# Block-sparse attention followed by a gated feed-forward layer: scores of two heads in two 64-row halves of TensorE, the mask as a 0/1 product, the hidden layer kept on the chip, and the two layers interleaved by token group

## The chip, the cores and the metric

One core of one Trainium2 chip runs the whole program. The metric is device time of one execution in microseconds (us), the median of several runs; nearly all runs of a kernel lie within 0.8% of its median. Every ratio below is the ratio of a kernel's fast runs to the fast runs of the kernel before, of the same rounds on the same chip, so it is not quite the ratio of the medians that are quoted. Differences in us between two experiments or to the changed kernel are differences of medians, and the experiments ran on three chips; where the ratios give a figure more than 1 us away, the text says so. A profile is one execution; its span is 1 to 2 us shorter than the timed run, and stage times below are read from profiles.

Engines: PE is TensorE (PEld its weight loads), DVE is VectorE, ACT is ScalarE, POOL is GpSimd, SP is SyncE, which here only issues transfers.

## The reference

Batch 4, 8 heads, 768 positions, head size 64. The mask works on blocks of 32 positions: neighbours, first and last block, and three sampled blocks per block row. The second layer is called MoE in the code, but it is one dense gated layer.

```python
scores = scale * np.matmul(q, k.transpose(0, 1, 3, 2))      # (4, 8, 768, 768)
mask = np.abs(blk_i - blk_j) <= 1
mask = mask | (blk_i == 0) | (blk_j == 0) | (blk_i == n_blocks - 1) | (blk_j == n_blocks - 1)
for qb in range(n_blocks):
    for kb in sampled_blocks[qb]:
        mask[qb*32:(qb+1)*32, kb*32:(kb+1)*32] = True
scores = np.where(mask, scores, -1e9)
attn = softmax(scores)                                      # written out in the reference
x = (attn @ v) as 3072 tokens x 512
h = x @ w_in                                                # 512 -> 2048
g = h * (1.0 / (1.0 + np.exp(-beta * h)))
return g @ w_out                                            # 2048 -> 512
```

Both kernels skip the maximum (the scores are small), sum each row of exp by a column of ones beside v, and compute the gate as 0.5 * h * (1 + tanh(beta*h/2)).

## The kernel before

One head at a time. q and k are transposed on PE into the first 64 rows of a tile; 24 more rows hold the block mask (-30000 for a masked block on the q side, a one-hot of the key's block on the k side). The score matmul thus contracts 88 rows and gives masked scores, and exp is all that follows.

```python
CROWS = D + NB                                   # 64 + 24
for kc in range(NKC):                            # 6 chunks of 128 keys
    sc = scores_pool.tile([P, S], FP32, tag="sc")
    nc.tensor.matmul(sc[:, 0:512], lhsT=ka[0:CROWS, kc*P:(kc+1)*P],
                     rhs=qa[0:CROWS, 0:512], start=True, stop=True)
    nc.tensor.matmul(sc[:, 512:S], lhsT=ka[0:CROWS, kc*P:(kc+1)*P],
                     rhs=qa[0:CROWS, 512:S], start=True, stop=True)
    nc.scalar.activation(out=et[:, kc, :], in_=sc, func=AF.Exp, bias=0.0, scale=SCALE)
```

The hidden layer is computed in two halves. "Front" matmuls of the first three token groups run between the heads; VectorE casts their result and it goes to DRAM. "Back" reads it again, takes tanh on ScalarE and the gate product on VectorE. In the source the rest of the layer stands after attention; in the trace 46 of the 96 tanh run before the last rows of attention are written.

```python
def emit_h_front(tg, ffc, h_pool):
    ...                                          # four matmuls of 512 columns into hp
    nc.vector.tensor_copy(out=hst, in_=hp)
    nc.sync.dma_start(out=h_dram[tg * N_FFC + ffc], in_=hst)

def emit_h_back(tg, ffc, g_sb):
    nc.sync.dma_start(out=hld, in_=h_dram[tg * N_FFC + ffc])
    nc.scalar.activation(out=t_sb, in_=hld, func=AF.Tanh, bias=0.0, scale=beta_h_sb[:, ffc:ffc+1])
    nc.vector.scalar_tensor_tensor(out=g_sb[:, ffc, :], in0=t_sb, scalar=1.0, in1=hld,
                                   op0=ALU.add, op1=ALU.mult)
```

The instructions are traced in this order, but the build's scheduler fixes each engine's queue with its own model of durations.

The softmax here doesn't subtract the row's maximum and nothing guards it: scores larger than these inputs give would overflow.

Of the kernel before, what the change touches and what calls it, by code (L numbers as in the profile page):

```python
# [9 lines left out]
FP32 = mybir.dt.float32  # L11
FP16 = mybir.dt.float16
AF = mybir.ActivationFunctionType
ALU = mybir.AluOpType

NEG = -30000.0
# [3 lines left out]
def kernel(  # L20
# [17 lines left out]
    NKC = S // P  # L38
    NQC = S // P
# [3 lines left out]
    N_DMC = D_MODEL // P  # L43
    N_FFC = D_FF // P
    SCALE = 1.0 / float(D) ** 0.5

    CROWS = D + NB

    n_bh = B * H
    N_TG = N_TOK // 512  # L50

    persist = ctx.enter_context(tc.tile_pool(name="persist", bufs=1))
    setup_pool = ctx.enter_context(tc.tile_pool(name="setup", bufs=1))
    dram_pool = ctx.enter_context(tc.tile_pool(name="dram", bufs=1, space=bass.MemoryType.DRAM))


    h_dram = dram_pool.tile([N_TG * N_FFC, P, 512], FP16, name="h_dram")

    identity = persist.tile([P, P], FP16, name="identity")
    make_identity(nc, identity)  # L60

    xT_sb = persist.tile([P, N_DMC, N_TOK], FP16, name="xT_sb")
    w_in_sb = persist.tile([P, N_DMC, D_FF], FP16, name="w_in_sb")
    w_out_sb = persist.tile([P, N_FFC, D_MODEL], FP16, name="w_out_sb")
    beta_h_sb = persist.tile([P, N_FFC], FP32, name="beta_h_sb")

    sb_i32 = setup_pool.tile([NB, 3], mybir.dt.int32, name="sb_i32")
# [3 lines left out]
    nc.sync.dma_start(out=sb_i32, in_=sb_lo)  # L71
    sb_f32 = setup_pool.tile([NB, 3], FP32, name="sb_f32")
    nc.vector.tensor_copy(out=sb_f32, in_=sb_i32)

    mask_blk = setup_pool.tile([NB, NB], FP32, name="mask_blk")
    nc.vector.memset(mask_blk, 1.0)
    nc.gpsimd.affine_select(out=mask_blk, in_=mask_blk, pattern=[[-1, NB]],
                            compare_op=ALU.is_ge, fill=0.0, base=1,
                            channel_multiplier=1)
    nc.gpsimd.affine_select(out=mask_blk, in_=mask_blk, pattern=[[1, NB]],  # L80
                            compare_op=ALU.is_ge, fill=0.0, base=1,
                            channel_multiplier=-1)
    nc.gpsimd.affine_select(out=mask_blk, in_=mask_blk, pattern=[[0, NB]],
                            compare_op=ALU.not_equal, fill=1.0, base=0,
                            channel_multiplier=1)
    nc.gpsimd.affine_select(out=mask_blk, in_=mask_blk, pattern=[[0, NB]],
                            compare_op=ALU.not_equal, fill=1.0, base=-(NB - 1),
                            channel_multiplier=1)
    nc.gpsimd.affine_select(out=mask_blk, in_=mask_blk, pattern=[[1, NB]],
                            compare_op=ALU.not_equal, fill=1.0, base=0,  # L90
                            channel_multiplier=0)
    nc.gpsimd.affine_select(out=mask_blk, in_=mask_blk, pattern=[[1, NB]],
                            compare_op=ALU.not_equal, fill=1.0, base=-(NB - 1),
                            channel_multiplier=0)
    iota_j = setup_pool.tile([NB, NB], FP32, name="iota_j")
    nc.gpsimd.iota(iota_j, pattern=[[1, NB]], base=0, channel_multiplier=0,
                   allow_small_or_imprecise_dtypes=True)
    for r in range(3):
        ind_r = setup_pool.tile([NB, NB], FP32, name=f"ind_{r}")
        nc.vector.tensor_scalar(out=ind_r, in0=iota_j, scalar1=sb_f32[:, r:r + 1],  # L100
                                scalar2=None, op0=ALU.is_equal)
        nc.vector.tensor_tensor(out=mask_blk, in0=mask_blk, in1=ind_r, op=ALU.max)

    mask_add16 = setup_pool.tile([NB, NB], FP16, name="mask_add16")
    nc.vector.tensor_scalar(out=mask_add16, in0=mask_blk, scalar1=1.0, scalar2=-NEG,
                            op0=ALU.subtract, op1=ALU.mult)

    with tc.tile_pool(name="setup_psum", bufs=1, space=bass.MemoryType.PSUM) as setup_psum:
        maskT_ps = setup_psum.tile([NB, NB], FP16, name="maskT_ps")
        nc.tensor.transpose(out=maskT_ps, in_=mask_add16, identity=identity[0:NB, 0:NB])  # L110
        maskT16 = setup_pool.tile([NB, NB], FP16, name="maskT16")
        nc.vector.tensor_copy(out=maskT16, in_=maskT_ps)  # L112

    beta_sb = setup_pool.tile([P, N_FFC], FP32, name="beta_sb")
    nc.scalar.dma_start(out=beta_sb, in_=moe_beta.rearrange("(c p) -> p c", p=P))
# [5 lines left out]
    weight_chunks = []  # L121
    for c in range(N_DMC):
        weight_chunks.append((w_in_sb[:, c, :], w_in_r[:, c, :], None,
                              "w_in_st", [P, D_FF]))
    for c in range(N_FFC // 2):
        weight_chunks.append((w_out_sb[:, 2 * c:2 * c + 2, :],
                              w_out_r[:, 2 * c:2 * c + 2, :], 0.5,
                              "w_out_st", [P, 2, D_MODEL]))
    wstage = ctx.enter_context(tc.tile_pool(name="wstage", bufs=2))

    NBUF = 3
    NEBUF = 2

    qaug_tiles = []
    kaug_tiles = []
    vaug_tiles = []
    et_tiles = []
    for i in range(NBUF):
        qa = persist.tile([P, S], FP16, name=f"qaug_{i}")
        ka = persist.tile([P, S], FP16, name=f"kaug_{i}")  # L140
        va = persist.tile([P, NKC, D + 1], FP16, name=f"vaug_{i}")
        nc.vector.tensor_copy(
            out=qa[D:CROWS, :].rearrange("p (i w) -> p i w", w=BLK),
            in_=maskT16[:, :].to_broadcast([NB, NB, BLK]),
        )
        nc.vector.memset(ka[D:CROWS, :], 1.0)
        nc.gpsimd.affine_select(out=ka[D:CROWS, :], in_=ka[D:CROWS, :],
                                pattern=[[1, NB], [0, BLK]],
                                compare_op=ALU.is_equal, fill=0.0, base=0,
                                channel_multiplier=-1)  # L150
        nc.vector.memset(va[:, :, D:D + 1], 1.0)
        qaug_tiles.append(qa)
        kaug_tiles.append(ka)
        vaug_tiles.append(va)
    for i in range(NEBUF):
        et = persist.tile([P, NKC, S], FP16, name=f"et_{i}")
        et_tiles.append(et)

    stage_pool = ctx.enter_context(tc.tile_pool(name="stage", bufs=2))
    xstage_pool = ctx.enter_context(tc.tile_pool(name="xstage", bufs=2))  # L160

    attn_psum_ctx = ExitStack()
    scores_pool = attn_psum_ctx.enter_context(
        tc.tile_pool(name="scores_psum", bufs=2, space=bass.MemoryType.PSUM))
    tp_pool = attn_psum_ctx.enter_context(
        tc.tile_pool(name="tp_psum", bufs=2, space=bass.MemoryType.PSUM))
    av_pool = attn_psum_ctx.enter_context(
        tc.tile_pool(name="av_psum", bufs=1, space=bass.MemoryType.PSUM))
    xtp_pool = tp_pool
    hf_pool = attn_psum_ctx.enter_context(  # L170
        tc.tile_pool(name="hf_psum", bufs=1, space=bass.MemoryType.PSUM))

    moe_sbuf = ctx.enter_context(tc.tile_pool(name="moe_sbuf", bufs=3))

    small_pool = ctx.enter_context(tc.tile_pool(name="small", bufs=4))

    xstage = None

    def emit_h_front(tg, ffc, h_pool):
        hp = h_pool.tile([P, 512], FP32, tag="hfp", name="hfp")  # L180
        for c in range(N_DMC):
            nc.tensor.matmul(hp,  # L182
                             lhsT=w_in_sb[:, c, ffc * P:(ffc + 1) * P],
                             rhs=xT_sb[:, c, tg * 512:(tg + 1) * 512],
                             start=(c == 0), stop=(c == N_DMC - 1))
        hst = moe_sbuf.tile([P, 512], FP16, tag="hst", name="hst")
        nc.vector.tensor_copy(out=hst, in_=hp)  # L187
        nc.sync.dma_start(out=h_dram[tg * N_FFC + ffc], in_=hst)

    def emit_h_back(tg, ffc, g_sb):  # L190
        hld = moe_sbuf.tile([P, 512], FP16, tag="hld", name="hld")
        nc.sync.dma_start(out=hld, in_=h_dram[tg * N_FFC + ffc])
        t_sb = moe_sbuf.tile([P, 512], FP16, tag="t_sb", name="t_sb")
        nc.scalar.activation(out=t_sb, in_=hld, func=AF.Tanh,  # L194
                             bias=0.0, scale=beta_h_sb[:, ffc:ffc + 1])
        nc.vector.scalar_tensor_tensor(out=g_sb[:, ffc, :], in0=t_sb,  # L196
                                       scalar=1.0, in1=hld,
                                       op0=ALU.add, op1=ALU.mult)

    def emit_o_unit(tg, tsub, o_pool, g_sb):  # L200
        op = o_pool.tile([P, D_MODEL], FP32, tag="op", name="op")
        for ffc in range(N_FFC):
            nc.tensor.matmul(op,  # L203
# [175 lines left out]
```

## Time and profile before

| | before |
|---|---|
| median time, first 3 runs | 362.66 us (361.95 to 363.61) |
| span of the profile | 361.5 us |
| first exp starts | 26.4 us |
| last rows of attention written | 233.7 us |

The first lines are from the profile's page: busy time of each engine, and the chain of work that ended last, by engine.

```profile
PE 326.7 (90%) x2785; PEld 184.5 (51%) x2785; DVE 238.1 (66%) x488; ACT 206.5 (57%) x289; POOL 4.9 (1%) x16
...
PE 80%; ACT 9%; DMA 5%; DVE 3%; issue 1%; SPq 0%; ACTq 0%
```

TensorE is busy for 90% of the time and is 80% of the chain.

The next lines are the page's costliest groups: line, engine, operation, what it writes from what, shapes and count, then busy us and mean ns of one, then idle time of the engine just before them and what ended it.

```profile
L194 ACT ACTIVATE t_sb<-hld,beta_h_sb 128x512 f16<-128x512 f16 x96 | 66.7, 720 | 66.6 <-DMA hld<-h_dram 39.6
L182 PE MATMUL hfp<-xT_sb,w_in_sb 128*128 128x512 f16 x384 | 100.7, 379 | 0.0
L203 PE MATMUL op<-w_out_sb,g_sb 128*128 128x512 f16 x384 | 84.7, 379 | 0.0
L272 ACT ACTIVATE et_142<-sc 128x768 f16<-128x768 f32 x96 | 70.8, 812 | 23.1 <-PE sc L269 17.9
...
L187 DVE CAST hst<-hfp 128x512 f16<-128x512 f32 x96 | 64.2, 685 | 9.2 <-PE hfp L182 5.2
```

ScalarE waits 39.6 us for the hidden layer to come back from DRAM, but ScalarE is not the engine that bounds.

The table of stretches follows: the stretch, its length, busy time of each engine with its number of instructions, granted clock, DMA share and GB/s.

```profile
0.00:26.40 26.40, 5.06 (x34) 3.57 (x35) 11.69 (x34) 1.33 (x2) 4.88 (x16) 1.00 0.91 271
26.40:90.00 63.60, 57.20 (x616) 37.31 (x615) 33.96 (x82) 47.15 (x63) 0.00 (x0) 0.97 0.56 148
90.00:217.00 127.00, 125.33 (x1391) 78.11 (x1388) 102.33 (x227) 109.55 (x157) 0.00 (x0) 1.00 0.66 172
```

In the first 26.4 us nothing much runs while transfers fill 91% of the DMA engines. From 90 to 217 us PE is full (125.33 of 127 us).

### The profile page before, as it was taken

To read this page: it belongs to the slowest core of one execution; us is meant where nothing else is said; L and a number is where in the kernel's file an instruction comes from. 1 tells how busy PE (TensorE), PEld (TensorE's weight loads), DVE (VectorE), ACT (ScalarE), POOL (GpSimd) and SP (SyncE) were. 2 spreads that over 40 slices of the span, in tenths; PEclk is the share of its full clock that TensorE was granted. 3 is DMA by queue.
4 is the path that set the end of the run, shared out by engine and by line. 5 is a ranking of instruction groups with operands and counts; after the bars stand their busy time and mean duration, and the time that the engine had idled before them with its cause. 6 is when DMAs were issued, how large, how long until landed. Compare 5 with 4: busy or idle time off the path is not lost.

```text
span 361.5 us, 7349 instructions
## 1 busy us (share of the span) xinstructions
PE 326.7 (90%) x2785; PEld 184.5 (51%) x2785; DVE 238.1 (66%) x488; ACT 206.5 (57%) x289; POOL 4.9 (1%) x16
## 2 busy tenths in 40 slices
PE   0329988989999999999999998999999999999995
PEld 0215655655566566566666655544444444444442
DVE  2465346555877977977887797725987977985121
ACT  0027686687889889788888977610452452443000
POOL 5000000000000000000000000000000000000000
PEclk9999989999999999999999999999999999999999
DMA  7894276655667666676666742233664754763212
GB/s 231 242 339 98 80 190 204 189 127 144 169 177 190 179 160 179 160 184 174 175 174 164 189 138 61 90 103 133 213 205 145 230 183 160 220 200 119 87 58 89
DMA packets 111303, 59.22 MB, mean 164 GB/s; under 512 B 81060, under 2 KB 105636, under 8 KB 110756
## 3 DMA queue, kind: packets, MB, share of 16 engines
q1 hardware_dynamic: 106452, 50.35, 50.1%
q10 hardware_dynamic: 4816, 8.40, 6.7%
q8 instruction: 22, 0.36, 0.4%
q14 instruction: 13, 0.11, 0.1%
HBM read 39.85 MB, written 18.87 MB: 162 GB/s over the span
## 4 chain that ended last, share of the span: by engine, by line
PE 80%; ACT 9%; DMA 5%; DVE 3%; issue 1%; SPq 0%; ACTq 0%
PE hfp L182 23%; PE op L203 23%; PE sc L266 12%; PE av L285 8%; PE tp L254 7%; ACT et_142 L272 6%; PE sc L269 5%; ACT et_141 L272 3%; DMA st_318<-in_q_dram 3%; DMA st_181<-in_k_dram 2%; PE xtp L304 2%; DVE xstage L294 1%; ACT t_sb L194 0%; SPq L71 0%; DVE recip L293 0%
## 5 line engine op out<-in xcount | busy, mean ns | idle before, releaser
L194 ACT ACTIVATE t_sb<-hld,beta_h_sb 128x512 f16<-128x512 f16 x96 | 66.7, 720 | 66.6 <-DMA hld<-h_dram 39.6
L182 PE MATMUL hfp<-xT_sb,w_in_sb 128*128 128x512 f16 x384 | 100.7, 379 | 0.0
L203 PE MATMUL op<-w_out_sb,g_sb 128*128 128x512 f16 x384 | 84.7, 379 | 0.0
L272 ACT ACTIVATE et_142<-sc 128x768 f16<-128x768 f32 x96 | 70.8, 812 | 23.1 <-PE sc L269 17.9
L272 ACT ACTIVATE et_141<-sc 128x768 f16<-128x768 f32 x96 | 70.3, 816 | 11.2 <-PE sc L269 11.0
L196 DVE SCALAR_TENSOR_TENSOR g_sb<-t_sb,hld 128x512 f16<-128x512 f16 x96 | 64.0, 684 | 11.8 <-ACT t_sb L194 11.5
L187 DVE CAST hst<-hfp 128x512 f16<-128x512 f32 x96 | 64.2, 685 | 9.2 <-PE hfp L182 5.2
L203 PEld LDWEIGHTS <-g_sb 128*128 128x128 f16 x384 | 37.6, 98 | 45.3
L182 PEld LDWEIGHTS <-w_in_sb 128*128 128x128 f16 x384 | 35.6, 97 | 35.4 <-issue 0.4
L208 DVE COPY osb<-op 128x512 f32<-128x512 f32 x24 | 16.5, 689 | 31.7 <-PE op L203 31.6
L285 PEld LDWEIGHTS <-et_142 128*128 128x128 f16 x576 | 29.2, 101 | 12.2 <-issue 1.7
L293 DVE RECIPROCAL recip<-av 128x6 f32<-128x6 f32 x32 | 6.3, 196 | 41.1 <-PE av L285 40.4
L285 PEld LDWEIGHTS <-et_141 128*128 128x128 f16 x576 | 26.3, 100 | 9.3 <-issue 2.5
L266 PE MATMUL sc<-qaug_120,kaug_121 88*128 88x512 f16 x66 | 25.8, 399 | 3.1 <-ACT et_142 L272 1.2
L266 PE MATMUL sc<-qaug_127,kaug_128 88*128 88x512 f16 x66 | 26.5, 410 | 2.1 <-ACT et_142 L272 1.2
L266 PE MATMUL sc<-qaug_134,kaug_135 88*128 88x512 f16 x60 | 23.2, 394 | 2.0 <-ACT et_142 L272 0.9
L269 PE MATMUL sc<-qaug_127,kaug_128 88*128 88x256 f16 x66 | 19.2, 291 | 0.0
L269 PE MATMUL sc<-qaug_120,kaug_121 88*128 88x256 f16 x66 | 18.8, 284 | 0.0
L294 DVE TENSOR_TENSOR xstage<-av,recip 128x384 f16<-128x384 f32 x32 | 17.6, 551 | 0.1
L269 PE MATMUL sc<-qaug_134,kaug_135 88*128 88x256 f16 x60 | 16.8, 281 | 0.0
L272 ACT ACT_TABLE_LOAD x1 | 1.3, 1283 | 22.4 <-DVE maskT_111 L112 22.4
L285 PE MATMUL av<-vaug_122,et_141 128*128 128x65 f16 x216 | 12.9, 203 | 0.0
(284 smaller groups left out, 260.7 us busy)
## 6 DMA issues: line engine op xcount, KB each, us to landing
h_dram<-hst SPq DMA_DIRECT2D x96, 128.0 KB, 1.9
hld<-h_dram SPq DMA_DIRECT2D x96, 128.0 KB, 2.3
out_dram<-osb SPq DMA_DIRECT2D x24, 256.0 KB, 2.0
w_in_st<-in_moe_w_in_dram ACTq DMA_DIRECT2D x4, 1024.0 KB, 7.1
w_out_st<-in_moe_w_out_dram ACTq DMA_DIRECT2D x8, 512.0 KB, 5.4
st_169<-in_q_dram SPq DMA_DIRECT2D x1, 192.0 KB, 8.8
st_181<-in_k_dram SPq DMA_DIRECT2D x1, 192.0 KB, 9.0
vst_193<-in_v_dram SPq DMA_DIRECT2D x1, 192.0 KB, 9.0
```

Source lines behind the costliest of these rows:

```text
L182: nc.tensor.matmul(hp, lhsT=w_in_sb[:, c, ffc * P:(ffc + 1) * P], rhs=xT_sb[:, c, tg * 512:(tg + 1) * 512], start=(c == 0), stop=(c == N_D ...
L187: nc.vector.tensor_copy(out=hst, in_=hp)
L194: nc.scalar.activation(out=t_sb, in_=hld, func=AF.Tanh, bias=0.0, scale=beta_h_sb[:, ffc:ffc + 1])
L196: nc.vector.scalar_tensor_tensor(out=g_sb[:, ffc, :], in0=t_sb, scalar=1.0, in1=hld, op0=ALU.add, op1=ALU.mult)
L203: nc.tensor.matmul(op, lhsT=g_sb[:, ffc, tsub * P:(tsub + 1) * P], rhs=w_out_sb[:, ffc, :], start=(ffc == 0), stop=(ffc == N_FFC - 1))
L208: nc.vector.tensor_copy(out=osb, in_=op)
L254: nc.tensor.transpose(out=tp[:, c, :], in_=st16[:, c, :], identity=identity[:, 0:P])
L266: nc.tensor.matmul(sc[:, 0:512], lhsT=ka[0:CROWS, kc * P:(kc + 1) * P], rhs=qa[0:CROWS, 0:512], start=True, stop=True)
L269: nc.tensor.matmul(sc[:, 512:S], lhsT=ka[0:CROWS, kc * P:(kc + 1) * P], rhs=qa[0:CROWS, 512:S], start=True, stop=True)
L272: nc.scalar.activation(out=et[:, kc, :], in_=sc, func=AF.Exp, bias=0.0, scale=SCALE)
L285: nc.tensor.matmul(av[:, qc, :], lhsT=pet[:, kc, qc * P:(qc + 1) * P], rhs=pva[:, kc, :], start=(kc == 0), stop=(kc == NKC - 1))
L294: nc.vector.tensor_tensor(out=xstage[:, :, (ph % 2) * D:(ph % 2 + 1) * D], in0=av[:, :, 0:D], in1=recip[:, :].to_broadcast([P, NQC, D]), o ...
```

## The change

Its intent: halve TensorE's work on scores by running two heads side by side in the upper and lower 64 rows of the array, halve the q and k transposes by transposing two heads at once, drop the DRAM round trip and the casts with it, and spread the feed-forward work over the attention of the next token group so that no engine idles. The mask rows no longer fit (two heads fill 128 rows), so the mask becomes a 0/1 product on VectorE after exp. The core of the diff:

```diff
-        sc = scores_pool.tile([P, S], FP32, tag="sc")
-        nc.tensor.matmul(sc[:, 0:512], lhsT=ka[0:CROWS, ...], rhs=qa[0:CROWS, 0:512], ...)
-        nc.tensor.matmul(sc[:, 512:S], lhsT=ka[0:CROWS, ...], rhs=qa[0:CROWS, 512:S], ...)
-        nc.scalar.activation(out=et[:, kc, :], in_=sc, func=AF.Exp, ...)
+        sc = sc_pool.tile([P, 2, 512], FP32, tag="sc", name="sc")
+        for i in range(kn):                       # 1 chunk of 512 queries, or 2 of 256
+            for hh in range(2):                   # head hh in rows hh*64 .. hh*64+63
+                nc.tensor.matmul(sc[:, hh, i*n:(i+1)*n],
+                                 lhsT=kT[hh*D:(hh+1)*D, (kc0+i)*P:(kc0+i+1)*P],
+                                 rhs=qT[hh*D:(hh+1)*D, q0:q0+n], start=True, stop=True)
+        et = et_pool.tile([P, 2, kn, n], FP16, tag="et", name="et")
+        nc.scalar.activation(out=et.rearrange("p h i n -> p h (i n)"), in_=sc, func=AF.Exp, ...)
+        for hh in range(2):
+            nc.vector.tensor_tensor(out=et[:, hh], in0=et[:, hh],
+                                    in1=mask_sb[:, kc0:kc0+kn, q0:q0+n], op=ALU.mult)
...
-        nc.vector.tensor_copy(out=hst, in_=hp)
-        nc.sync.dma_start(out=h_dram[tg * N_FFC + ffc], in_=hst)
-        nc.sync.dma_start(out=hld, in_=h_dram[tg * N_FFC + ffc])
-        nc.scalar.activation(out=t_sb, in_=hld, func=AF.Tanh, ...)
-        nc.vector.scalar_tensor_tensor(out=g_sb[:, ffc, :], in0=t_sb, scalar=1.0, in1=hld, ...)
+        nc.scalar.activation(out=t_sb[:, 0:n], in_=hp[:, 0:n], func=AF.Tanh, ...)
+        nc.vector.scalar_tensor_tensor(out=g[:, f, 0:n], in0=t_sb[:, 0:n], scalar=1.0,
+                                       in1=hp[:, 0:n], op0=ALU.add, op1=ALU.mult)
...
+    # beta: loaded by ScalarE's queue after the sampled blocks, scaled on VectorE
+    nc.scalar.dma_start(out=sb_i32, in_=sb_lo)
+    nc.scalar.dma_start(out=beta_sb, in_=moe_beta.rearrange("(c p) -> p c", p=P))
+    nc.vector.tensor_scalar(out=beta_h_sb, in0=beta_sb, scalar1=0.5, ...)
+    # weights: cast to fp16 by the transfer itself, issued from GpSimd
+    nc.gpsimd.dma_start(out=w_in_sb[:, :, i*512:(i+1)*512], in_=w_in_r[:, :, i*512:(i+1)*512])
...
+    tiles = [(0, 0, 256), (0, 256, 512), (1, 0, 512), (1, 512, 256),
+             (2, 0, 256), (2, 256, 512), (3, 0, 512), (3, 512, 256)]
+    groups = [[0], [1], [2], [3, 4], [5], [6], [7]]
+    # attention steps of group g are interleaved with the MoE steps of group g-1
```

Attention now goes by tiles of 256 or 512 queries. PSUM holds two score tiles of two banks, one bank for the weighted sums, and three banks shared by transposes, hidden layer and output.

## The prediction

> **What bounds the kernel now.** TensorE. The page gives PE 326.7 of 361.5 us busy (90%), the chain that ended last is 80% PE. VectorE has 238.1 us, ScalarE 206.5 us. The first exp runs only at 26.35 us (timeline), behind 192 KB loads that took about 9 us beside the weight loads. Start-to-start in the timeline: 512-column matmul 0.216 us, AV matmul 0.036, 128-column q/k transpose 0.066. PE work by these: MoE 768 x 0.216 = 166 us, scores 192 x 0.32 = 61, AV 1152 x 0.036 = 42, q/k transposes 384 x 0.066 = 25, xtp 6: 300 us.
>
> **What the change does on PE.** Two heads share a transpose: 25 to about 12 us. Score pairs run side by side: 288 matmuls of 512 columns' worth (or twice as many of 256), 61 us in series, 31 if the halves overlap fully. The Trainium skill, "TensorE: Matmul & The Clock Gate" (Part 3), measured 3.07x for four row tiles, so two should overlap nearly; but "TensorEngine Tiling (Array Packing)" (Key Properties) says changing the tiling mode drains the array, and this happens twice per score step, 144 steps. I allow 0.05 to 0.15 us per step (an estimate): scores 40 to 52 us. No run so far shows it. New PE sum: about 270 to 280 us.
>
> **VectorE.** Removed: 96 hst casts (64 us), weight casts (10 us). Added: 288 fp16 products of 512 columns; from 551 ns for 384 fp32 columns, and two elements a cycle for fp16 ("VectorE: DVE Perf Modes", perf-mode tier table), I estimate 0.42 us each, 0.34 back to back: about 100 us. Sum about 240 to 260 us: no relief.
>
> **ScalarE.** 144 exps of 1024 columns, from 0.812 us per 768 an estimated 1.03 us each (148 us busy), tanh about 60, output copies 14: about 220 us. The DRAM spill goes, but DMA was not the bound.
>
> **By stage.** All three engines are near balance, so I expect coupling losses: a bank of the hidden layer is held through tanh and gate product, and three banks serve h, o and transposes. Start to first exp about 17 us; group 0 (no MoE, VectorE-bound) 20; group 1 about 33; four full groups 47 to 50 each (first half VectorE-bound by gate plus mask, second half PE-bound); group 6 about 37; tail MoE of 256 tokens about 17. Sum about 316 us. The gain is the saved PE work (about 25 us), the earlier start (about 9 us) and fewer stalls.
>
> **Prediction: 315 us, 8 in 10 between 294 and 337.** Faster by over 2%: 0.95; within 2%: 0.03; slower: 0.02.
>
> **What would show the steps right or wrong.** Pairs of score matmuls starting within about 0.02 us of each other, with a visible gap after them before the next full-height matmul; mask products near 0.42 us; exp near 1.03 us; busy time PE 270 to 290, VectorE 240 to 260, ScalarE 210 to 230; steady groups of 47 to 50 us with VectorE above 90% in their first halves; first exp near 17 us.
>
> **What would make it wrong.** Mask products at one element a cycle (0.68 us: 75 us more on VectorE, no gain left); score halves that do not overlap or drains of 0.3 us a switch (20 to 40 us more); weight loads issued from GpSimd that come late and stall the first MoE group; or, the other way, no drain and good overlap, near 295 us.

## More of the kernel before

Note that busy time counts a matmul from its start to its modelled end, so it holds pipeline latency as well as work.

A matmul of 512 columns shows 379 ns because of that latency. Between the starts of two neighbours there are only 216 ns, and that is what a full PE pays.

## The result and the profile after

| | before | after |
|---|---|---|
| median, same rounds | 362.31 us (361.23 to 363.61) | 353.34 us (352.87 to 353.95) |
| ratio | | 0.9749 (0.9722 to 0.9776) |
| span of the profile | 361.5 us | 351.1 us |
| first exp starts | 26.4 us | 26.5 us |

The change is faster by 2.5%. The prediction was 315 us, at most 337: the direction was right and most of the gain did not come. The page of the kernel after, the lines that answer to those above:

```profile
PE 302.9 (86%) x2670; PEld 152.1 (43%) x2670; DVE 250.6 (71%) x666; ACT 216.4 (62%) x281; POOL 9.7 (3%) x26
...
PE 61%; ACT 16%; DVE 11%; DMA 7%; issue 4%; ACTq 0%
...
L215 ACT ACTIVATE et<-sc 128x1024 f16<-128x1024 f32 x144 | 143.1, 1033 | 86.4 <-PE sc L209 85.3
L218 DVE TENSOR_TENSOR et<-et,mask_sb 128x512 f16<-128x512 f16 x288 | 108.9, 420 | 30.6 <-ACT et L215 28.5
L292 PE MATMUL op<-w_out_sb,g 128*128 128x512 f16 x384 | 97.4, 380 | 0.0
...
L209 PE MATMUL sc<-qT,kT 64*128 64x256 f16 (+1 forms) x384 | 63.1, 351 | 11.0 <-ACT et L215 8.0
...
L135 DVE TENSOR_SCALAR beta_h_sb<-beta_sb 128x16 f32<-128x16 f32 x1 | 0.2, 174 | 16.5 <-DMA beta_sb<-in_moe_beta_dram 16.5
```

VectorE and ScalarE are as predicted, product by product: 420 ns, 1033 ns, 250.6 and 216.4 us busy. The last line is one that I did not foresee: a 174 ns instruction with 16.5 us of idle VectorE in front of it.

By stage. A group ends where its last attention rows are written to `xT_sb`; group 0 has no MoE work beside it, groups 2 to 5 are the four full ones, the tail is the MoE work of the last group. The scheduler runs some scores of a group before the last rows of the one before, so the borders are a little soft. First what the table of stretches gives (columns as above):

```profile
0.00:26.50 26.50, 2.08 (x19) 1.78 (x20) 5.42 (x19) 1.28 (x1) 9.70 (x26) 1.00 1.07 230
26.50:61.10 34.60, 29.11 (x235) 16.46 (x232) 31.12 (x90) 20.18 (x22) 0.00 (x0) 0.95 0.80 219
61.10:92.70 31.60, 28.54 (x346) 17.64 (x344) 27.82 (x83) 23.52 (x35) 0.00 (x0) 1.00 0.37 120
92.70:295.00 202.30, 192.30 (x1707) 90.61 (x1707) 155.78 (x401) 139.67 (x176) 0.00 (x0) 1.00 0.16 52
295.00:331.10 36.10, 35.61 (x274) 16.35 (x272) 23.80 (x61) 22.93 (x31) 0.00 (x0) 1.00 0.08 30
331.10:351.10 20.00, 15.23 (x99) 9.29 (x97) 6.70 (x16) 8.82 (x19) 0.00 (x0) 0.97 0.11 40
```

| stage | predicted | measured | difference |
|---|---|---|---|
| start to first exp | 17 | 26.5 | +9.5 |
| group 0 | 20 | 34.6 | +14.6 |
| group 1 | 33 | 31.6 | -1.4 |
| four full groups | 192 (4 x 48) | 202.3 | +10.3 |
| group 6 | 37 | 36.1 | -0.9 |
| tail | 17 | 20.0 | +3.0 |
| sum | 316 | 351.1 | +35.1 |

Two thirds of the miss lie in the first 61 us, and a bit under a third in the four full groups.

What PE's work was worth. A change of mode is a change of the rows or columns of the array that a matmul uses, from all 128 to 64 or back. This table takes the median time between the starts of neighbouring matmuls of one kind, from the trace, times their number in the program. It holds no waits.

| work on PE | before | after |
|---|---|---|
| MoE | 768 x 0.216 = 166 us | 704 x 0.216 + 128 x 0.109 = 166 us |
| scores | 192 x (0.216 + 0.109) = 62 us | 144 x 0.219 = 32 us |
| changes of mode | 48 x (0.09 + 0.10) = 9 us | 124 x (0.10 + 0.10) = 25 us |
| weighted sums | 1152 x 0.033 = 38 us | 1152 x 0.032 = 37 us |
| q and k transposes | 384 x 0.056 = 22 us | 192 x 0.056 = 11 us |
| transposes of x, mask | 5 us | 5 + 2 us |
| sum | 302 us | 278 us |
| span less sum | 59 us | 73 us |

The 32 us for scores take every pair of halves as running together. In the trace 25 of the 192 pairs start more than 17 ns apart, which adds at most 4 us (an estimate: 12 x 0.216 and 13 x 0.109). So PE's work fell by 20 to 24 us, the span by 10. All that the change was to gain beside PE's work, an earlier start and fewer stalls, did not come: what is not PE work was 59 us and is 69 to 73. Of the 20 to 24 us, 20 come from the transposes and only the rest from the scores, as the kernel before changes mode too: its transposes of one head use 64 columns of the array (`128*64` in the page's terms), in 48 blocks. The median spacing from a MoE matmul to such a transpose is 308 ns where 216 is the plain one, and from the transpose to a MoE matmul 152 where 56 is. The transposes of two heads use all 128 columns, and in the kernel after the spacing from a MoE matmul to them is 216 ns.

The line of the table that needs showing is the change of row mode. These are start times of single matmuls in the trace of the kernel after (us, output, rows x columns); a pair of scores starts together:

```
95.471  hp  128 x 512
95.686  hp  128 x 512     0.215 after the one before
95.998  sc   64 x 512     0.312: 0.10 more than 0.216, the mode changes
96.001  sc   64 x 512     its partner, 0.003 later
96.321  hp  128 x 512     0.320: 0.10 more, and back
```

In the trace, 167 of the 192 pairs of score matmuls start within 17 ns of each other (median 3 ns). Over the kernel PE changes to 64 rows 124 times and back 124 times. The median spacing from a 128-row matmul of 512 columns to a score matmul is 312 ns, and from a pair of 512 columns back to a MoE matmul 319 ns, where 216 is the plain spacing.

The start. The timeline's first column is the start, the second the duration; what stands in brackets is idle time before it, and who ended it. First two lines of the kernel before, whose beta load is the first on its queue:

```profile
0.81 0.42 ACTq L115 DMA_DIRECT2D beta_sb<-in_moe_beta_dram  x1
...
4.21 0.15 DVE L116 TENSOR_SCALAR beta_h_sb<-beta_sb 128x16 f32<-128x16 f32 x1
```

Then the kernel after. The last fence line is from the waits of the transfer queue (total us, times, longest).

```profile
2.25 0.40 ACTq L85 DMA_DIRECT2D beta_sb<-in_moe_beta_dram  x1
...
4.42 0.15 DVE L88 CAST sb_f_100<-sb_i_96 24x3 f32<-24x3 int32 x1 [4.42 <-DMA sb_i_96<-in_sampled_blocks_dram]
...
5.30 1.06 SPq L69 DMA_DIRECT2D qst<-in_q_dram  x1
...
21.09 0.37 SPq L69 DMA_DIRECT2D vst<-in_v_dram  x1
21.09 0.17 DVE L135 TENSOR_SCALAR beta_h_sb<-beta_sb 128x16 f32<-128x16 f32 x1 [16.52 <-DMA beta_sb<-in_moe_beta_dram]
21.18 0.55 DVE L180 CAST k_152<-kst 128x768 f16<-128x768 f32 x1
...
SPq L69 <- DMA beta_sb<-in_moe_beta_dram: 14.7, 1, 14.7
```

The first k, q and v had landed by 8.0 us. But VectorE's queue had the scaling of beta (8 KB, needed only at the first tanh, 61.8 us) before the first cast, and beta, issued at 2.25 us behind four other loads and beside 8 MB of weights, landed at 21.07 us. In the same instant SyncE issues the third v load, which had waited for beta as well.

Why a v load waits for beta stands in the packed trace, in the operands of the transfers. Each transfer signals its landing on a semaphore (a counter that others can wait for), and the built program gives eight of them in turn to the transfers of SyncE and ScalarE. The third v load has the same one as beta (number 102) and waits for it before it is issued. In the run beta_first below, beta shares number 100 with the third k load, and there that load waits.

### The profile page after: what moved, and what is told of

The parts are those of the page before. It is cut to its first block, busy times and chain, and to the rows that moved or that the text cites. A ratio compares the mean times of both kernels' runs of the same rounds, so it can differ in the third digit from the quotient of the medians.

```text
span 351.1 us, 6634 instructions
## 1 busy us (share of the span) xinstructions
PE 302.9 (86%) x2670; PEld 152.1 (43%) x2670; DVE 250.6 (71%) x666; ACT 216.4 (62%) x281; POOL 9.7 (3%) x26
## 4 chain that ended last, share of the span: by engine, by line
PE 61%; ACT 16%; DVE 11%; DMA 7%; issue 4%; ACTq 0%
PE op L292 20%; PE hp L273 16%; ACT et L215 11%; PE av L239 9%; PE sc L209 8%; DMA beta_sb<-in_moe_beta_dram 5%; ACT t_sb L278 4%; DVE et L218 4%; PE tp L185 4%; DVE g L280 3%; PE xtp L253 3%; DVE xst L245 2%; DMA vst<-in_v_dram 2%; PE mk L166 1%; DVE recip L244 0%
## 5 line engine op out<-in xcount | busy, mean ns | idle before, releaser
L215 ACT ACTIVATE et<-sc 128x1024 f16<-128x1024 f32 x144 | 143.1, 1033 | 86.4 <-PE sc L209 85.3
L218 DVE TENSOR_TENSOR et<-et,mask_sb 128x512 f16<-128x512 f16 x288 | 108.9, 420 | 30.6 <-ACT et L215 28.5
L292 PE MATMUL op<-w_out_sb,g 128*128 128x512 f16 x384 | 97.4, 380 | 0.0
L273 PE MATMUL hp<-xT_sb,w_in_sb 128*128 128x512 f16 (+1 forms) x448 | 94.0, 349 | 0.8 <-DVE g L280 0.2
L278 ACT ACTIVATE t_sb<-hp,beta_h_sb 128x512 f16<-128x512 f32 (+1 forms) x112 | 69.4, 640 | 16.5 <-PE hp L273 16.2
L280 DVE SCALAR_TENSOR_TENSOR g<-t_sb,hp 128x512 f16<-128x512 f16 (+1 forms) x112 | 67.1, 608 | 8.7 <-ACT t_sb L278 7.6
L209 PE MATMUL sc<-qT,kT 64*128 64x256 f16 (+1 forms) x384 | 63.1, 351 | 11.0 <-ACT et L215 8.0
L239 PEld LDWEIGHTS <-et 128*128 128x128 f16 x1152 | 45.2, 100 | 27.2 <-DVE xst L245 14.8
L273 PEld LDWEIGHTS <-w_in_sb 128*128 128x128 f16 x448 | 39.9, 97 | 36.1 <-issue 8.4
L292 PEld LDWEIGHTS <-g 128*128 128x128 f16 x384 | 31.7, 97 | 34.3 <-issue 8.2
L244 DVE RECIPROCAL recip<-av 128x2 f32<-128x2 f32 (+1 forms) x64 | 11.1, 173 | 20.3 <-PE av L239 20.1
L135 DVE TENSOR_SCALAR beta_h_sb<-beta_sb 128x16 f32<-128x16 f32 x1 | 0.2, 174 | 16.5 <-DMA beta_sb<-in_moe_beta_dram 16.5
L239 PE MATMUL av<-va_73,et 128*128 128x65 f16 x216 | 9.9, 199 | 1.2 <-DVE xst L245 1.0
L239 PE MATMUL av<-va_77,et 128*128 128x65 f16 x216 | 9.3, 196 | 1.8 <-DVE xst L245 1.8
L239 PE MATMUL av<-va_79,et 128*128 128x65 f16 x216 | 9.9, 199 | 0.7 <-DVE xst L245 0.5
## 6 DMA issues: line engine op xcount, KB each, us to landing
beta_sb<-in_moe_beta_dram ACTq DMA_DIRECT2D x1, 8.0 KB, 18.8
```

The source lines that it names most:

```text
L209: nc.tensor.matmul(sc[:, hh, i * n:(i + 1) * n], lhsT=kT[hh * D:(hh + 1) * D, (kc0 + i) * P:(kc0 + i + 1) * P], rhs=qT[hh * D:(hh + 1) * D ...
L215: nc.scalar.activation(out=et.rearrange("p h i n -> p h (i n)"), in_=sc, func=AF.Exp, bias=0.0, scale=SCALE)
L218: nc.vector.tensor_tensor(out=et[:, hh], in0=et[:, hh], in1=mask_sb[:, kc0:kc0 + kn, q0:q0 + n], op=ALU.mult)
L239: nc.tensor.matmul(av[:, qc, :], lhsT=et[:, hh, i, qc * P:(qc + 1) * P], rhs=va[:, hh, kc, 0:D + 1], start=(kc == 0), stop=(kc == NC - 1))
L273: nc.tensor.matmul(hp[:, 0:n], lhsT=w_in_sb[:, c, f * P:(f + 1) * P], rhs=xT_sb[:, c, t0:t0 + n], start=(c == 0), stop=(c == NPAIR - 1))
L278: nc.scalar.activation(out=t_sb[:, 0:n], in_=hp[:, 0:n], func=AF.Tanh, bias=0.0, scale=beta_h_sb[:, f:f + 1])
```

## Experiments

Theories. **T1:** a change of row mode costs about 0.10 us on PE each way, and gives back what running two heads side by side saves. **T2:** the first 61 us are lost to beta's landing and to weights that compete with the first loads. **T3:** in the full groups the mask products make VectorE the bound of each group's first half. Rivals stand in the expectations. Each result is correct unless the text says otherwise; "changed kernel" is the kernel after, 353.34 us, ratio 0.9749.

### 1. beta_late: the start, VectorE's queue alone

```diff
-    nc.vector.tensor_scalar(out=beta_h_sb, in0=beta_sb, scalar1=0.5, ...)
+    # after group 0's steps; the read of xT_sb keeps the scheduler from moving it up
+    nc.vector.scalar_tensor_tensor(out=beta_t, in0=xT_sb[:, 0, 0:N_FFC], scalar=0.0,
+                                   in1=beta_sb, op0=ALU.mult, op1=ALU.add)
+    nc.vector.tensor_scalar(out=beta_h_sb, in0=beta_t, scalar1=0.5, ...)
```

The false dependency is there so that the build's scheduler cannot put the scaling back at the head of VectorE's queue. No run moves the line alone.

> The scaling of beta on VectorE is made to depend on the first finished attention rows, so it no longer stands at the head of VectorE's queue. Theory (queue blocked by one small load): the first exp moves from 26.5 us to about 12 us and the total from 351 to about 340 us. Rival (the start is bound by the transfers themselves, since the third v load was seen to land at 27.6 us and its cast stands before the mask in the queue): the first exp comes earlier, but the first masked step stays near 33 to 36 us and the total falls by less than 4 us.

Measured: 352.98 us (351.8 to 353.93), ratio 0.975: no gain. The first exp did move, from 26.5 to 16.7 us, but group 0 ended at 59.6 us in place of 61.1. The rival was right. The third v load was again issued only when beta had landed (21.73 us), landed at 28.1 us, and its cast stands in VectorE's queue before the building of the wide mask.

### 2. w_late: the weights held back

```diff
+        if b == 0 and j == 2:       # a small write that waits for the v load of pair 2
+            nc.gpsimd.tensor_copy(out=w_in_sb[:, 0, i*512:i*512+1], in_=sts[2][:, 0, 0:1])
+        if b == 0 and j == 3:       # the same for w_out, pair 3
+            nc.gpsimd.tensor_copy(out=w_out_sb[:, i*4, 0:1], in_=sts[2][:, 0, 0:1])
```

> The weight transfers start only when the v load of the third pair (w_in) and of the fourth pair (w_out) have landed. The scaling of beta still stands first in VectorE's queue. Both theories: beta lands earlier than 21 us because less is in flight. If the start is bound by what competes with the loads, the total falls by 8 to 14 us (to about 338 to 343); if the queue order alone matters, by the amount by which beta lands earlier, which I put at 5 to 10 us. A stall of the first MoE group on late weights would show as matmul waits on w_in near 45 to 60 us and would eat the gain.

Measured: 344.88 us, ratio 0.9519, 8.5 us less than the changed kernel. Beta landed at 13.5 us, the third v load at 16.6. Both sides of the expectation give about this number, so this run alone does not tell them apart. No stall on weights was seen: group 1 took 31.7 us.

### 3. both_late

> Both edits together. Theory (two causes in series, queue and transfers): first exp near 11 us, end of group 0 near 45 us in place of 61, total near 338 us. If this is no better than the better of the two alone by more than 1 us, the two edits remove the same wait.

Measured: 339.79 us, ratio 0.937, 13.5 us less than the changed kernel, and more than the 0.4 and 8.5 us of the two alone. Group 0 ended at 47.4 us (I expected 45). The waits stand one behind the other: with one taken away, the other is still there. The third v load still waits for beta in this run, but beta lands at 13.89 us. The table of stretches for this run shows that nothing after the start was touched; these are start, group 0, group 1 and the full groups:

```profile
0.00:13.50 13.50, 2.28 (x20) 1.69 (x20) 5.63 (x18) 1.28 (x1) 3.67 (x18) 1.00 0.81 234
13.50:47.40 33.90, 27.85 (x234) 15.94 (x231) 30.85 (x91) 20.10 (x21) 7.09 (x16) 0.80 1.07 267
47.40:79.60 32.20, 29.17 (x348) 17.91 (x345) 28.36 (x85) 24.01 (x35) 0.00 (x0) 1.00 0.65 163
79.60:281.90 202.30, 192.32 (x1707) 90.58 (x1707) 155.69 (x402) 139.68 (x176) 0.00 (x0) 1.00 0.16 52
```

Group 0 still takes 33.9 us, with VectorE busy for 30.85 of them: it holds the building of the wide mask and the casts and copies of the later pairs beside its products. My 20 us were too few for it whatever beta does. (TensorE's granted clock in it was 0.80, 0.95 in the changed kernel.)

### 4. beta_first: two lines change places

```diff
-    nc.scalar.dma_start(out=sb_i32, in_=sb_lo)
     nc.scalar.dma_start(out=beta_sb, in_=moe_beta.rearrange("(c p) -> p c", p=P))
+    nc.scalar.dma_start(out=sb_i32, in_=sb_lo)
```

> Only the two small loads on ScalarE's queue change places: beta is issued first, at about 0.8 us, before much else is in flight. The run beta_late showed that the third v load is issued only when beta has landed, whatever VectorE does. Theory (beta's landing holds both VectorE's queue and, through the third v load, the wide mask): beta lands before 8 us, the third v load is issued by then and lands near 22 us in place of 27.6, total 4 to 8 us less than the changed kernel, 345 to 349. Rival (the weights in flight alone set it): within 2 us of the changed kernel.

Measured: 346.39 us, ratio 0.9567, 7 us less than the changed kernel, inside the expected band. Beta landed at 7.15 us; the third k load, which now shares beta's semaphore, went out at 7.17 us (4.60 in the changed kernel) and the third v load at 9.56, in place of 21.09. When the third v landed is missing from this trace. So 8 KB, issued 1.4 us earlier, are worth 2%.

### 5. one_mode: no change of row mode, no two heads side by side

Each head's k^T stands in its own 128-row tile with zeros in the other head's rows; the right-hand side is the pair's q^T. To fit in SBUF there is one buffer less for v and k and one less for exp.

```diff
-            lhsT=kT[hh*D:(hh+1)*D, (kc0+i)*P:(kc0+i+1)*P],
-            rhs=qT[hh*D:(hh+1)*D, q0:q0+n],
+            lhsT=kT[hh][:, (kc0+i)*P:(kc0+i+1)*P],     # rows of the other head are zero
+            rhs=qT[:, q0:q0+n],
```

> Scores of both heads by full-height matmuls: each head's k^T stands in its own tile with the other head's 64 rows zero, so PE never changes its row mode for them; the two 512-column matmuls of a step then run one after the other (0.432 us) where they ran together (about 0.22 us) with two changes of mode (0.10 us each, read from the trace of the change: 0.312 and 0.318 us between starts where 0.216 is the plain spacing). Theory (the changes of mode give back all that running side by side saves): total within 1% of the changed kernel's 353 us, perhaps 1 to 4 us slower for 16 more copies of 0.55 us on VectorE. Rival (the halves do pay and the loss is elsewhere): 144 steps x 0.2 us = 28 us slower, about 380 us.

Measured: 353.54 us (352.62 to 354.68), ratio 0.9758 against 0.9749: the same time. In this trace the spacing from a MoE matmul to a score matmul is 216 ns again, and two score matmuls of 512 columns follow each other at 216 ns. The four full groups took 201.8 us (202.3 in the changed kernel). By the spacings its scores take 62 us, where the changed kernel pays 32 and 25 us for the changes, and up to 4 for the split pairs. Running two heads side by side is worth nothing here as it is interleaved. That is T1. The comparison is not quite clean: one_mode has fewer buffers and more copies, and VectorE is busy for 161.70 us in its full groups (155.78 in the changed kernel):

```profile
95.30:297.10 201.80, 193.46 (x1707) 105.36 (x1706) 161.70 (x414) 139.82 (x176) 0.00 (x0) 1.00 0.16 54
```

### 6. mixed_mode: changes of mode without the overlap

As one_mode, but head 0 uses 64 rows and head 1 all 128.

```diff
-            lhsT=kT[hh][:, (kc0+i)*P:(kc0+i+1)*P],
-            rhs=qT[:, q0:q0+n],
+            lhsT=kT[hh][0:(D, P)[hh], (kc0+i)*P:(kc0+i+1)*P],
+            rhs=qT[0:(D, P)[hh], q0:q0+n],
```

> As one_mode, but head 0 goes through the upper 64 rows alone while head 1 uses all 128 rows: no two matmuls run side by side, and there are two changes of row mode per block of scores as in the changed kernel (more where a step has four matmuls). Theory (a change of mode costs about 0.10 us on a TensorE that bounds): 144 steps x 0.2 us, plus 48 steps x 0.2 us for those of four matmuls, is 38 us of TensorE time, total 20 to 40 us above one_mode's 353.5, about 375 to 390. Rival (the 0.1 us seen in the trace is hidden elsewhere): under 8 us above.

Measured: 380.57 us (one of five runs was slow and is left out of the ratio, 1.0503), 27.0 us above one_mode. The trace has 192 changes each way, so one change and back costs 27.0 / 192 = 0.14 us of the whole time. The spacing shows about 0.2 us of PE's; the difference is probably time in which PE would have waited anyway, which no run separates. This is the disputed cost by itself, and it is real.

### 7. four_banks: fewer changes of mode

Two score steps write one tile of four banks, so their matmuls stand together; the tile has one buffer where there were two of two banks.

```diff
-        tc.tile_pool(name="sc_psum", bufs=2, space=bass.MemoryType.PSUM))
+        tc.tile_pool(name="sc_psum", bufs=1, space=bass.MemoryType.PSUM))
...
-                sc = sc_pool.tile([P, 2, 512], FP32, tag="sc", name="sc")
+                sc4 = sc_pool.tile([P, 2, 2, 512], FP32, tag="sc", name="sc")   # two steps
```

> Two score steps share one tile of four PSUM banks (one buffer in place of two of two banks), so the row mode changes for 80 blocks of scores in place of 144. Theory (each block costs two changes of 0.10 us on a bound TensorE): 64 x 0.2 = 13 us of TensorE time go, total down by 6 to 13 us. Rival (the lost double buffer makes TensorE wait for exp): the score matmuls wait for exp longer by as much or more, total within 2 us or slower.

Measured: 363.35 us, ratio 1.0074: 10 us slower (12 by the ratios). The theory's number fell here. First, the scheduler had already put neighbouring steps together in places: the changed kernel has 124 changes each way and not 144, this one 94, so only 30 x 0.2 = 6 us were to be had. Second, the lost double buffer probably costs more: group 1 took 36.7 us in place of 31.6 and the four full groups 205.6 in place of 202.3, with PE busy less in them (190.39 for 192.30 us), that is, waiting more. TensorE's granted clock was lower as well, 0.94 in group 1 and 0.98 in the full groups where it had been 1.00; no run separates that share.

### 8. no_mask: the products left out

The two `tensor_tensor` lines are taken out. The result is wrong (relative error 0.82).

> Gives a wrong result on purpose: the 288 mask products on VectorE (109 us busy) are left out, all else of the changed kernel stays. Theory (TensorE bounds the four full groups, with some stalls from coupling): each full group falls from 48.6 to 52.4 us to about 47 to 49, the first 61 us by about 5 us, total down by 12 to 18 us to about 338. Rival (the mask products on VectorE are what bounds): total down by 35 us or more. Rival (VectorE has nothing to do with it): under 4 us.

Measured: 339.96 us, ratio 0.9416, 13.4 us less (12 by the ratios), inside the band. These are group 0 and the four full groups:

```profile
26.90:54.10 27.20, 22.34 (x224) 12.17 (x221) 21.87 (x58) 15.47 (x17) 0.00 (x0) 1.00 1.11 323
...
86.00:279.70 193.70, 187.93 (x1709) 90.36 (x1707) 92.92 (x210) 139.25 (x175) 0.00 (x0) 1.00 0.17 55
```

Without the 109 us of products group 0 is 7.4 us shorter and the full groups 8.6 us. T3 says where those 8.6 us should lie. These are the two halves of group 2, hidden layer first, output second; first in the changed kernel, then without the products:

```profile
92.70:118.20 25.50, 23.81 (x189) 11.20 (x189) 24.56 (x58) 21.59 (x29) 0.00 (x0) 1.00 0.24 76
118.20:143.80 25.60, 25.21 (x237) 11.69 (x234) 15.53 (x42) 12.68 (x16) 0.00 (x0) 1.00 0.29 94
...
86.00:110.00 24.00, 23.54 (x192) 10.86 (x190) 17.32 (x32) 21.73 (x29) 0.00 (x0) 1.00 0.31 95
110.00:134.30 24.30, 24.30 (x240) 11.67 (x237) 7.45 (x20) 12.60 (x16) 0.00 (x0) 1.00 0.28 97
```

In the first half VectorE is busy for 24.56 of 25.5 us, in the second PE for 25.21 of 25.6. But with VectorE down to 17.32 us the first half still takes 24.0. Over all four groups, cut where the first output matmul starts, the first halves take 99.8 us with the products and 97.9 without, the second halves 102.5 and 95.8. So T3 is not borne out: VectorE is 87 to 96% busy in the first halves, but PE (88 to 95%) and ScalarE (85 to 93%) are close, and most of what the products cost lies in the second halves. One wait of PE that goes with them is that of the weighted sums, which have one bank, for VectorE to scale the sums before (`xst`); this is the line for the full groups of the changed kernel (total us, times, longest), and without products the same view has no such line:

```profile
PE av L239 <- DVE xst L245: 4.3, 10, 1.2
```

That the products delay `xst` in VectorE's queue is the likely reading; no run tests it alone.

### 9. add_mask: the mask back in the contraction

The mask rows of the kernel before, in the changed kernel: head 0 in rows 0 to 63 with its mask in rows 64 to 87, head 1 in rows 64 to 127 with its mask in rows 0 to 23 and zeros between. One head per matmul, no products, no wide mask, no change of mode.

```diff
-            lhsT=kT[hh*D:(hh+1)*D, (kc0+i)*P:(kc0+i+1)*P],
-            rhs=qT[hh*D:(hh+1)*D, q0:q0+n],
+            lhsT=kT[hh][0:(D + NB, P)[hh], (kc0+i)*P:(kc0+i+1)*P],
+            rhs=qT[hh][0:(D + NB, P)[hh], q0:q0+n],
...
-            nc.vector.tensor_tensor(out=et[:, hh], in0=et[:, hh], in1=mask_sb[...], op=ALU.mult)
```

> The mask as 24 more rows of the contraction, as the kernel before had it, one head per matmul, full row mode; all else of the changed kernel stays. TensorE time for scores 0.432 us per step, the same as overlap plus two changes of mode; VectorE loses the products (109 us) and the building of the wide mask (6 us) and gets 32 more copies of 0.55 us. Theory: as no_mask, total about 336 to 342 us with a right result. If it is no faster than the changed kernel, the products cost nothing on the chain.

Measured: 348.79 us, ratio 0.967: a miss, 4.6 us gained (3 by the ratios) where 11 to 17 were expected. The cause is the start: the first exp came at 39.6 us. In VectorE's queue the casts of later v loads stood before the mask rows (it waited 12.0 us in all for three v loads, 7.0 us for the longest, which ended at 35.8 us). I take this order to come from ten memsets that I had put ahead of the mask's first steps on GpSimd. That is not shown: best1, which has the mask first, has no memsets there, but its source also builds the mask before it prepares the first pair. From the first exp on the run took 308.7 us against 324.6 us of the changed kernel (351.1 less 26.5), and the four full groups 196.2 against 202.3:

```profile
95.80:292.00 196.20, 191.97 (x1709) 105.36 (x1707) 106.19 (x233) 138.81 (x175) 0.00 (x0) 1.00 0.17 57
```

### 10. moe_last: attention first, all of MoE after it

```diff
-        per = len(backlog) / max(1, len(a_steps))
+        per = 0.0
...
-        for m in backlog:
-            m()
...
-        backlog = moe_steps(t0, sum(tiles[ti][2] for ti in members))
+        backlog += moe_steps(t0, sum(tiles[ti][2] for ti in members))
```

> All MoE steps are issued after all attention steps (the scheduler of the build may still move a few forward). Theory (interleaving pays because attention alone is bound by VectorE and ScalarE): attention ends near 190 to 205 us with TensorE under 60% busy, MoE takes 170 us more, total 360 to 375 us, 2 to 6% slower than the changed kernel. Rival (interleaving brings nothing): within 1%.

Measured: 381.34 us, ratio 1.0563: 28 us slower (29.5 by the ratios), more than expected. Attention and MoE one after the other:

```profile
26.90:206.50 179.60, 132.92 (x1825) 85.79 (x1822) 171.11 (x536) 136.84 (x144) 0.00 (x0) 0.90 0.32 96
206.50:380.50 174.00, 168.65 (x831) 81.62 (x829) 68.45 (x113) 83.65 (x136) 0.00 (x0) 0.99 0.10 37
```

Attention alone is bound by VectorE (171.11 of 179.6 us; TensorE's granted clock there was 0.90). So the interleaving is the part of the change without which the products on VectorE would have made it a loss.

### 11. before_nospill: one part of the change, in the kernel before

```diff
-        nc.vector.tensor_copy(out=hst, in_=hp)
-        nc.sync.dma_start(out=h_dram[tg * N_FFC + ffc], in_=hst)
+        nc.vector.tensor_copy(out=h_ring[tg % 4][:, ffc, :], in_=hp)
...
-        nc.sync.dma_start(out=hld, in_=h_dram[tg * N_FFC + ffc])
+        hld = g_sb[:, ffc, :]                       # gated in place
```

> The kernel before with one part of the change alone: the hidden layer stays in SBUF (four groups, gated in place) and no longer goes to DRAM and back. Theory (the transfers were not on the chain; ScalarE's waits for them cost nothing): within 1% of the kernel before, 358 to 364 us. Rival (the round trip was part of what the change saved): over 2% faster, under 355 us.

Measured: 362.2 us against 362.1, ratio 1.0003 (0.9961 to 1.0046). The round trip through DRAM cost nothing, although ScalarE had waited 39.6 us for it in total. ScalarE did not stop waiting: it stood idle for 61.5 us before these tanh in place of 66.6, now 41.7 us of it for VectorE's cast, which this run keeps. Idle time of an engine that does not bound cost nothing here.

### 12. best1: what the runs taught, in one kernel

add_mask with beta issued first, the weights held back, the mask built before the first pair is prepared, and each buffer's mask rows filled just before its first use (the last is shown):

```diff
+    def emit_rows(i):                               # called in the first use of buffer i
+        nc.gpsimd.memset(kz_tiles[i][1][0:D, :], 0.0)
+        nc.gpsimd.memset(qz_tiles[i][1][0:D, :], 0.0)
+        for hh, r in ((0, D), (1, 0)):
+            nc.scalar.copy(out=kz_tiles[i][hh][r:r + NB, :], in_=oh_flat)
+            nc.vector.tensor_copy(out=qz_tiles[i][hh][r:r + NB, :], in_=maskx)
```

> A version meant to beat both: add_mask (mask rows in the contraction, full row mode, no products on VectorE), with beta issued first, weights held back until the v loads of the third and fourth pair, and the mask rows of each buffer filled just before its first use. Theory: from its first exp to its end add_mask took 308.7 us (348.3 less 39.6); with a first exp near 13 to 16 us this gives 320 to 328 us, 7 to 9% below the changed kernel. Above 335 us one of the gains does not add to the others.

Measured: 330.56 us (329.87 to 333.26), ratio 0.9143: 31.5 us below the kernel before and 22.8 us below the changed kernel, correct. It is 2.6 us above the expected band, since the first exp came at 20.3 us. Its start, group 0, group 1 and full groups:

```profile
0.00:20.30 20.30, 4.83 (x33) 3.44 (x33) 11.37 (x28) 6.26 (x7) 13.77 (x38) 1.00 0.91 296
20.30:45.50 25.20, 19.74 (x203) 13.51 (x202) 21.44 (x56) 21.63 (x24) 4.57 (x6) 1.00 1.15 244
45.50:76.40 30.90, 30.21 (x348) 19.56 (x347) 14.00 (x41) 24.39 (x37) 0.00 (x0) 1.00 0.54 150
76.40:272.70 196.30, 192.07 (x1710) 105.36 (x1708) 106.32 (x234) 138.88 (x175) 0.00 (x0) 1.00 0.17 57
```

PE is busy for 98% of the full groups. The two 64-row halves, the headline of the change, are not in this kernel.

## Why the prediction was right or wrong

**Right.** TensorE bounds the kernel before. The DRAM round trip was not on the chain (before_nospill, 1.0003). The sizes of the new instructions: mask product 420 ns (0.42 predicted), exp 1033 ns (1.03), VectorE 250.6 us (240 to 260), ScalarE 216.4 us (210 to 230). The rule for the product, two 16-bit elements a cycle for `tensor_tensor` in SBUF, is that of the Trainium skill, "VectorE: DVE Perf Modes", perf-mode tier table (its column is bf16), and the trace agrees: 420 ns for 512 fp16 columns, where the `tensor_tensor` that scales 256 fp32 columns takes 422. Halves of a pair overlap: partners start 3 ns apart, as the skill's "TensorE: Matmul & The Clock Gate", Part 3, lets expect. The saved PE work ("about 25 us") nearly came, 20 to 24 us by the spacings, though mostly from the transposes. Group 1, group 6 and the busy shares in a full group (VectorE above 90% in the first half of three of the four, then PE) were right too.

**Wrong: "Start to first exp about 17 us", "the earlier start (about 9 us)".** It measured 26.5. The first loads were early, as I thought. What I missed was a small load in front of the queue: VectorE idle for 16.5 us before the scaling of beta. I read the order in the diff and did not ask what each queue would hold first and what would be in flight beside it. That is the step that failed: the path to the first exp ran through beta's landing, and not through the first k and q loads. The runs settle it: with VectorE's wait for beta and the competing weights both taken away, 13.5 us come back; with the beta load issued first, 7; with the VectorE wait alone, nothing, because the third v load waits for beta's semaphore too. I had named weights that come late as a risk; they came early (w_in by 24.4 us, needed at 61) and held up the loads that were needed first.

**Wrong: "group 0 (no MoE, VectorE-bound) 20".** VectorE-bound was right (31.12 of 34.6 us busy), the size was not: VectorE's work there is 37 products (13.9 us), the wide mask (6.9), casts and copies of q, k and v (8.8) and smaller pieces. The prediction gives no sum behind its 20, so which of these it left out cannot be told. Mending the start hardly changes it (33.9 us); without products it takes 27.2.

**Mis-sized: "I allow 0.05 to 0.15 us per step ... scores 40 to 52 us".** The skill's "TensorEngine Tiling (Array Packing)", Key Properties, says that changing the mode drains the array and gives no size. It measured 0.10 us each way, 0.20 us per block, 124 blocks: 25 us, so scores cost 32 + 25 = 57 us (up to 61 with the split pairs) where the kernel before paid 62. one_mode shows the sum: without overlap and without changes the time is the same to 0.1%.

**Mis-sized: "four full groups 47 to 50 each".** They took 202.3 / 4 = 50.6. With the products left out they took 48.4. "First half VectorE-bound by gate plus mask" is not what the runs show: without the products the first halves became 1.9 us shorter and the second halves 6.7. The dearer changes of mode fall here too: 89 of the 124, 18 us at 0.20 each, where the middle of my allowance, 0.10 us for each of 96 steps, is 10. Together that is more than the 10.3 us missed, and no run separates the two. The tail took 3 us more than predicted; no run looked into it.

**Wrong: "busy time PE 270 to 290" as a test.** The page gives 302.9. I compared a sum of start-to-start spacings with busy time, which holds latency; the sum from spacings is 278 us (282 with the split pairs), at the upper edge of my 270 to 280. My own number for before (300 against 326.7 busy) should have warned me.

**Wrong: "and fewer stalls".** What is not PE work was 59 us and is 69 to 73. The step behind it, that time falls with PE work and some of the rest falls as well, failed on the rest: the start did not get shorter, VectorE took over as the bound of group 0, and 8.6 us of the full groups hung on the products.

**What stays open.** How much of PE's 0.2 us per block is hidden in other waits (0.14 us on the total in mixed_mode). How the miss in the full groups divides between products and changes of mode. Why the tail is 20 us. How far a version with 64-row halves and all score steps of a pair in one block would get: it would need more PSUM than is free, and four_banks shows what giving up the second buffer costs.

## What to carry to other kernels

Two 64-row matmuls side by side save 0.22 us per pair of 512 columns, and a change of row mode there and back costs 0.20 us of TensorE: by these two numbers row halves pay only where several pairs stand in one block, and not one pair between full-height matmuls. No run here has such a block without another loss. What the change saved on PE came mostly from transposing two heads at once: 31 us with the changes of mode before, 11 after. When work is moved from a bound engine to another, do not take the fullest engine of a stage for its bound: here VectorE was 87 to 96% busy in the first halves of the full groups, yet taking the products away shortened mainly the second halves. The mask as 24 more rows of the contraction was better (196.2 us for the full groups against 202.3). Before trusting an early start, look up what each engine's queue holds first, when its operand lands, and which transfers share its semaphore: here 8 KB held two queues for 15 us, and issuing it 1.4 us earlier gave 2%.

## What the Trainium skill lacked or had wrong

- "TensorEngine Tiling (Array Packing)", Key Properties, says that changing the tiling mode drains TensorE, without a size. Here the spacing rose from 216 to 312 ns into 64-row mode and from 216 to 319 ns out of it; 192 such changes and back added 27.0 us to a kernel. Transposes in 64-column mode show it too: 308 for 216 ns on the way in, 152 for 56 on the way out.
- The same page promises up to 2x for a contraction of 64 rows ("Theoretical Speedup"), and "TensorE: Matmul & The Clock Gate", Part 3, gives measured speedups; neither says that between full-height matmuls the gain for a pair of 512 columns is used up by the changes of mode. Here two heads side by side and one after the other took 353.34 and 353.54 us.
- "DMA: Bandwidth & Descriptors" gives 512 B as the smallest transfer for line rate (Specifications). A time for a small load beside large ones is not there: 8 KB in 4-byte elements took 18.8 us to land beside 8 MB of weights, and 6.3 us when issued 1.4 us earlier, before the weights.
- None of the pages that I read warns that the order of an engine's queue in the built program can put an instruction before all others whose operand lands long after theirs: VectorE idled 16.5 us before the scaling of beta, while the first k, q and v had landed by 8.0 us.
- None of the pages that I read says that one transfer's issue can wait for the landing of an unrelated one with which it shares a completion semaphore in the built program. Here the third v load had beta's and went out when beta landed: at 21.09 us against a landing at 21.07, and at 21.73 against 21.71 in beta_late.
